# Splitting the first key load, loading small factors as rows and dropping zero rows in a fused attention and mixing kernel

## The chip, the cores and the metric

The program runs on one core of one Trainium2 chip. The metric is the device time of one execution in microseconds (us). A core has five engines that run their own lists of instructions in order: TensorE (PE; its weight loads are shown apart as PEld), VectorE (DVE), ScalarE (ACT), GpSimd (POOL) and SyncE (SP), which here only issues transfers. ScalarE issues a few transfers too.

## The reference

Three layers follow one another on batch B = 2, sequence S = 768, width 512:

```python
# 1. attention in hash buckets: 8 heads of 64, proj is 64 x 6
q_bits = (einsum('bhsd,dk->bhsk', q, proj) > 0)        # k_bits likewise
mask = q_bucket[:, :, :, None] == k_bucket[:, :, None, :]
scores = where(mask, scale * q @ k^T, -1e9)
x = softmax(scores) @ v                                # heads side by side
# 2. four attention experts of 64, causal, the two best per token, weighted
out += mask * w[:, :, kk] * (softmax(causal(q_e @ k_e^T)) @ v_e @ wo[e])
# 3. mixing with the token before
xk = mu_k * x + (1 - mu_k) * x_prev;  xr = mu_r * x + (1 - mu_r) * x_prev
k = max(xk @ w_k, 0);  out = sigmoid(xr @ w_r) * (k * k @ w_v)
```

## The kernel before

The tokens are cut into 12 tiles of 128 (6 per batch). For each tile the kernel makes the hash attention over 8 heads (`lsh_steps`), the experts (`moe_steps`) and the mixing (`mix_steps`). All numbers are split into a high and a low float16 part, and a product is made of two or three float16 products that add up in PSUM.

**Keys.** `key_steps` (from line 457) loads the keys of a group of four heads in two halves of two heads (`half(j)`), 384 KB each. ScalarE makes the high part and VectorE the low part into the tile `nak`, GpSimd puts a copy of the scaled keys into the first 64 columns of each 128 in the tile `nbk`. `turn` (line 338) transposes `nak` on TensorE in groups of six blocks of 128 x 128, and ScalarE and VectorE evict the results into `y2`. `hash_` multiplies `y2` with the projection (`hash_signs`) and `mark` writes 12 columns per block into `nbk`: a large number where a bit differs, else zero. The other 52 columns are filled with zeros by GpSimd. `nbk` is then transposed into `y1`. Queries go the same way (`query_steps`, tiles `naq`, `nbq`, `x2`, `x1`). A score is the sum of a product of `x1` with `y1` and one of `x2` with `y2`, each over 128 rows and twice 384 columns.

**Constants.** The projection is loaded twice, into rows 0 to 63 and 64 to 127 of `pr32`. The mixing factors `muk` and `mur` (128 x 4 each) are loaded with the partition as the inner index of memory, so every element is a piece of 4 bytes. They are first used when the first tile comes to the mixing, long after the start.

**Order.** The program is recorded first (class `Program`, line 151): every call of an engine becomes an operation, and consecutive TensorE calls of one step become one group. Then `issue` (line 203) makes all calls in the order of a table, `ORDER`, which holds one number per operation (2,594) and stands compressed in the source; `HOMES` holds the buffer of every tile. Both were written by a planner outside. As all calls go through line 208, the profile shows that line for all; the tiles' names tell them apart. Each engine takes its instructions from this order; SyncE and ScalarE issue their transfers in it.

The first transfers in the table of before are, on ScalarE's queue, the constants, the projection, `muk`, `mur`, the projection again and later `ties`; on SyncE's queue the queries of tile 0, three of the four first key halves, a weight load (128 KB of wq), the fourth key half, and more weight loads.

Of the kernel before, what the change touches and what calls it, by code (L numbers as in the profile page):

```python
# [42 lines left out]

KE, QE = {(0, 0): "va", (0, 1): "va"}, {}
# [191 lines left out]
def tile_lsh_moe_mix(  # L236
# [18 lines left out]
    G = 4  # L255
# [3 lines left out]
    NB2, NB3, NB4, NX2 = 40, 13, 2, 4  # L259

# [45 lines left out]
    nc.scalar.dma_start(pr32[0:64, :], proj)  # L306
    nc.scalar.dma_start(pr32[64:128, :], proj)
# [88 lines left out]
    def split_d(src, dst, sc, nm):  # L396
# [5 lines left out]
        top = raw[:, :, 1]  # L402
        nc.gpsimd.tensor_scalar(top.bitcast(F32), top.bitcast(F32), REBIAS, 1.0, op0=OP.mult, op1=OP.mult)
        w = dps(f"wd_{nm}", [P, n])
        u = w.bitcast(U32)
        nc.scalar.activation(u, raw.bitcast(U8)[:, :, 3], AF.Copy, bias=-15.5 / 32, scale=1.0 / 32)
        nc.vector.scalar_tensor_tensor(u, top, 3, u, op0=OP.logical_shift_left, op1=OP.bitwise_or)
        nc.vector.scalar_tensor_tensor(u, top, 0x80000000, u, op0=OP.bitwise_and, op1=OP.bitwise_or)
# [48 lines left out]
    def key_steps(b, g):  # L457
# [28 lines left out]
        def hash_():  # L486
# [24 lines left out]
    def query_steps(i):  # L511
# [16 lines left out]
        def hash_():  # L528
# [4 lines left out]
            turn(x1, nb.rearrange("p h c -> p (h c)"), f"x1_{i}", i in QD, QE.get(i, "vv"))  # L533
# [23 lines left out]
    def softmax(Sv, n, scale, sm, bias, nm, masked=None, by_pe=None):  # L557
# [6 lines left out]
        if masked:  # L564
            nc.vector.tensor_scalar(dst, Sv, masked, None, op0=OP.min, op1=OP.min, accum_out=bias)
            nc.vector.tensor_scalar(bias, bias, scale, None, op0=OP.mult)
        else:
            nc.vector.tensor_scalar(dst, Sv, -scale, None, op0=OP.mult, op1=OP.min, accum_out=bias)
        nc.scalar.activation(Pt, Pt, AF.Exp, bias=bias, scale=-scale if masked else -1.0, accum_out=sm)
        hi_part(hi_engine(), PHL[:, :n], Pt)  # L570
        lo_part("p", PHL[:, n:], Pt, PHL[:, :n])
        if by_pe:
            nk = n // P
            for j, eng in enumerate(by_pe):
                pt = dps(f"tp{j}_{nm}").bitcast(F16)[:, :n]
                for c in range(nk):
                    nc.tensor.transpose(pt[:, c * P:(c + 1) * P], PHL[:, j * n + c * P:j * n + (c + 1) * P], ident16)
                o = PT[:, j * nk:(j + 1) * nk, :]
                pt = pt.rearrange("p (t s) -> p t s", s=P)
                if eng == "a":  # L580
                    nc.scalar.activation(o, pt, AF.Copy)
                else:
                    nc.vector.tensor_copy(o, pt)
            return PT
        nc.sync.dma_start_transpose(PT, PHL)
        return PT
# [6 lines left out]
    def lsh_steps(i, LAG):  # L593
        b, t0 = divmod(i, NT)
        st = {"pt": {}}

        def score(h):
# [13 lines left out]
            st["pt"][h] = softmax(Sp[:, :, :HS], S, -0.125 / (SQ * SK), st["sm"][:, h:h + 1],  # L611
                                  st["mx"][:, h:h + 1], f"{i}_{h}", MASKED, SD.get((i, h)))
# [413 lines left out]
```

## Time and profile before

| | us |
|---|---|
| median of 3 runs | 457.49 (456.91 to 458.01) |
| profiled execution | 457.76 |
| its span (first to last instruction) | 455.9 |
| PE busy | 419.4 (92%) |
| PEld busy | 319.4 (70%) |
| DVE busy | 348.9 (77%) |
| ACT busy | 351.3 (77%) |
| POOL busy | 323.9 (71%) |

The profile is of one execution. Busy time is an average over stages that are bound by different engines, so the stages and the waits have to be read beside it. The granted TensorE clock is 1.00 in most stretches and lower in 30 to 60 us; its mean over the span is 0.985.

### The profile page before, as it was taken

The page shows a single profiled execution, that of the slowest core. Times are in us where ns is not written, and L with a number is a line of the kernel's source. Part 1 is how long each engine was busy: PE and PEld are TensorE (multiplying, and loading weights), DVE is VectorE, ACT ScalarE, POOL GpSimd, SP SyncE. Part 2 cuts the span into 40 slices and gives each one's busy share as a digit, 9 for nine tenths or more (in the row PEclk, how much of TensorE's full clock was granted, in tenths as well). Part 3 has the DMA queues.
Part 4 walks back from the last instruction along what each step waited for, and adds up shares of the span by engine and source line. Part 5 has one row for each costly group of instructions (what it writes and reads, how often), then busy time and mean ns, then how long its engine had stood idle before and what let it go on. Part 6 is the DMA issues. An engine that isn't in the chain of part 4 may idle for free.

```text
span 455.9 us, 15155 instructions
## 1 busy us (share of the span) xinstructions
PE 419.4 (92%) x6080; PEld 319.4 (70%) x6080; DVE 348.9 (77%) x994; ACT 351.3 (77%) x678; POOL 323.9 (71%) x321
## 2 busy tenths in 40 slices
PE   2765788899999999999999999999999999999996
PEld 2643566678767788687877778777768679866662
DVE  3899999999999789999787778867758537761513
ACT  4798999999999889689968978988597766552311
POOL 5599899999878876979989578689567844253020
PEclk9996799999999999999999999999999999999999
DMA  8999989899999999978999969997979975162003
GB/s 226 237 264 228 188 205 196 176 216 201 212 214 199 189 160 199 207 155 175 187 161 193 167 130 196 155 179 123 193 133 139 180 134 130 33 138 47 24 1 138
DMA packets 227158, 75.55 MB, mean 166 GB/s; under 512 B 218512, under 2 KB 222736, under 8 KB 227088
## 3 DMA queue, kind: packets, MB, share of 16 engines
q1 hardware_dynamic: 225584, 74.48, 84.3%
q8 instruction: 47, 0.77, 0.7%
q10 hardware_dynamic: 1504, 0.11, 0.3%
q14 instruction: 23, 0.19, 0.1%
HBM read 22.14 MB, written 3.15 MB: 55 GB/s over the span
## 4 chain that ended last, share of the span: by engine, by line
PE 66%; DVE 17%; DMA 6%; issue 5%; ACT 4%; POOL 1%; SPq 0%; DVEq 0%; ACTq 0%; POOLq 0%
PE h L208 13%; PE v L208 12%; PE s L208 8%; PE x L208 8%; PE r L208 6%; DVE P L208 5%; PE qk L208 5%; DMA PT<-PHL 3%; PE se L208 3%; PE vg L208 3%; PE o L208 3%; PE y L208 3%; DVE x L208 1%; DMA k<-in_k_dram 1%; DVE y L208 1%
## 5 line engine op out<-in xcount | busy, mean ns | idle before, releaser
L208 POOL TENSOR_TENSOR PHL<-P,PHL 128x768 f16<-128x768 f32 x96 | 159.4, 1672 | 26.8 <-ACT PHL L208 18.2
L208 DVE TENSOR_SCALAR_CACHE_REDUCE P<-s 128x768 f32<-128x768 f32 x96 | 90.9, 949 | 11.6 <-PE s L208 8.5
L208 ACT ACTIVATE P<-P,mx 128x768 f32<-128x768 f32 x96 | 89.0, 928 | 5.7 <-DVE mx L208 4.7
L208 PE MATMUL s<-y,x 128*128 128x384 f16 x384 | 78.2, 332 | 3.7 <-DVE P L208 2.4
L208 PE MATMUL h<-mk,WK 128*128 128x128 f16 x1152 | 74.5, 219 | 0.2 <-DVE x L208 0.2
L208 PEld LDWEIGHTS <-WK 128*128 128x128 f16 x1152 | 67.5, 98 | 6.0 <-issue 1.1
L208 PE MATMUL x<-v,PT 128*128 128x64 f16 x1728 | 63.5, 194 | 2.8 <-DMA PT<-PHL 1.4
L208 PEld LDWEIGHTS <-PT 128*128 128x128 f16 x1728 | 59.1, 99 | 8.3 <-DMA PT<-PHL 2.1
L208 ACT ACTIVATE PHL<-P 128x768 f16<-128x768 f32 x72 | 59.6, 837 | 5.7 <-DMA PT_m<-PHL_m 1.7
L208 PEld LDWEIGHTS <-x 128*128 128x128 f16 x480 | 38.7, 99 | 26.4 <-issue 7.0
L208 PE MATMUL v<-WV,k2h 128*128 128x512 f16 x192 | 57.1, 379 | 0.0
L208 POOL TENSOR_TENSOR PHL_m<-P_m,PHL_m 128x512 f16<-128x512 f32 (+2 forms) x24 | 34.6, 1452 | 8.1 <-ACT PHL_m L208 7.5
L208 PE MATMUL qk<-xT,WQK 128*128 128x128 f16 x576 | 36.3, 219 | 1.0 <-DVE xT L208 0.5
L208 PE MATMUL v<-WV,k2l 128*128 128x512 f16 x96 | 36.4, 379 | 0.0
L208 PEld LDWEIGHTS <-WQK 128*128 128x128 f16 x576 | 33.3, 98 | 2.8 <-issue 0.9
L208 PE MATMUL r<-WR,mr 128*128 128x512 f16 x144 | 35.0, 379 | 0.0
L208 POOL TENSOR_TENSOR mk<-m32k,mk 128x512 f16<-128x512 f32 x12 | 15.0, 1247 | 24.0 <-ACT mk L208 24.0
L208 DVE SCALAR_TENSOR_TENSOR h<-h,t 128x512 f32<-128x512 f32 x24 | 16.6, 693 | 19.5 <-ACT t L208 19.4
L208 ACT ACTIVATE t<-h 128x512 f32<-128x512 f32 x24 | 14.1, 586 | 17.1 <-PE h L208 17.1
L208 PEld LDWEIGHTS <-k2h 128*128 128x128 f16 x192 | 16.9, 98 | 13.0 <-DVE nbq L208 0.3
L208 ACT ACTIVATE P_m<-P_m,bias_m 128x512 f32<-128x512 f32 (+2 forms) x24 | 19.7, 822 | 7.4 <-DVE P_m L208 7.1
L208 POOL TENSOR_SCALAR PHL<-P 128x768 f16<-128x768 f32 x24 | 20.7, 863 | 4.4 <-ACT P L208 4.0
(146 smaller groups left out, 866.3 us busy)
## 6 DMA issues: line engine op xcount, KB each, us to landing
raw_k<-in_moe_w_k_dram SPq DMA_DIRECT2D x8, 512.0 KB, 4.2
raw_v<-in_moe_w_v_dram SPq DMA_DIRECT2D x8, 512.0 KB, 4.7
q<-in_q_dram SPq DMA_DIRECT2D x12, 256.0 KB, 4.7
k<-in_k_dram SPq DMA_DIRECT2D x8, 384.0 KB, 5.4
v<-in_v_dram SPq DMA_DIRECT2D x8, 384.0 KB, 4.9
out_dram<-e SPq DMA_DIRECT2D x12, 256.0 KB, 2.6
raw_r<-in_moe_w_r_dram SPq DMA_DIRECT2D x4, 512.0 KB, 4.6
PT<-PHL SPq DMA_TRANSPOSE x88, 4.3
```

The lines of the kernel that those rows point to most:

```text
L208: getattr(getattr(self.nc, engine), method)(*[real(a) for a in args], **{k: real(a) for k, a in kw.items()})
```

## The change

1. The first half of the keys (batch 0, group 0, half 0) is loaded, split into its high part and into its low part head by head: two transfers of 192 KB, two activations and two VectorE instructions in place of one each.
2. The projection is loaded once, through a view that repeats it.
3. `mu_k` and `mu_r` are loaded as four rows of 128 numbers each into one tile of eight rows, transposed on TensorE in one float32 product, and copied into one tile `mus`, of which `muk` and `mur` are the halves.
4. The keys' tiles are no longer filled with zeros. The transposes of `nbk` and `nbq` on TensorE take 76 columns (64 + 12) of each block, their evictions write 76 partitions, and the score products of `x1` and `y1` run over 76 rows.
5. `ORDER` and `HOMES` are new, for 2,590 operations. The first transfers in the new table are, on ScalarE's queue, the projection, the constants, `ties`, the rows of `mu_k`, then four activations (second, first and third key load used, the queries between), then the rows of `mu_r`; on SyncE's queue the second half of group 0's keys, the first half of group 1's, the queries of tile 0, the second half of group 1's, the two pieces of the first half of group 0's, then a weight load (wv), the queries of tile 1 and further weight loads.

Two switches, `PAIR` (empty) and `PRELU` (False), add branches that aren't taken; they are left out below, as are the tables.

```diff
+    KR = D + 2 * NB
...
-    nc.scalar.dma_start(pr32[0:64, :], proj)
-    nc.scalar.dma_start(pr32[64:128, :], proj)
+    nc.scalar.dma_start(pr32, proj.unsqueeze(0).to_broadcast([2, D, NB]))
...
-    muk = cp.tile([P, NC], F32, name="muk")
-    mur = cp.tile([P, NC], F32, name="mur")
+    mus = cp.tile([P, 2 * NC], F32, name="mus")
+    muk, mur = mus[:, :NC], mus[:, NC:]
...
-        nc.scalar.dma_start(muk, mu_k.rearrange("(c p) -> p c", p=P))
-        nc.scalar.dma_start(mur, mu_r.rearrange("(c p) -> p c", p=P))
+        rows = sp.tile([P, P], F32, tag="b2", bufs=NB2, name="mu_rows")
+        nc.scalar.dma_start(rows[0:NC, :], mu_k.rearrange("(c p) -> c p", p=P))
+        nc.scalar.dma_start(rows[NC:2 * NC, :], mu_r.rearrange("(c p) -> c p", p=P))
+        pt = dps("tr_mu", [P, P])
+        nc.tensor.transpose(pt[:, :2 * NC], rows[0:2 * NC, :], ident32[0:2 * NC, 0:2 * NC])
+        nc.vector.tensor_copy(mus, pt[:, :2 * NC])
...
-    def turn(dst, src, nm, by_dma=False, engs="vv"):
+    def turn(dst, src, nm, by_dma=False, engs="vv", kr=P):
...
-                nc.tensor.transpose(pt[j][:, c * P:(c + 1) * P], src[:, (j * hn + c) * P:(j * hn + c + 1) * P], ident16)
-            o, pj = dst[:, j * hn:(j + 1) * hn, :], pt[j].rearrange("p (n s) -> p n s", s=P)
+                nc.tensor.transpose(pt[j][:kr, c * P:(c + 1) * P], src[:, (j * hn + c) * P:(j * hn + c) * P + kr], ident16)
+            o, pj = dst[:kr, j * hn:(j + 1) * hn, :], pt[j][:kr].rearrange("p (n s) -> p n s", s=P)
...
-            LOADS.dma_start(k32, k[b, h0 + 2 * j:h0 + 2 * j + 2].rearrange(
-                "h (p t) d -> p h t d", t=NT))
...
-            kh = na[:, :, :, D:]
-            hi_part("a", kh, k32, SK)
-            lo_part("v", na[:, :, :, :D], k32, kh, SK)
+            cuts = [slice(r, r + 1) for r in range(2)] if (b, g, j) == (0, 0, 0) else [slice(0, 2)]
+            for r in cuts:
+                LOADS.dma_start(k32[:, r], k[b, h0 + 2 * j + r.start:h0 + 2 * j + r.stop].rearrange(
+                    "h (p t) d -> p h t d", t=NT))
+            for r in cuts:
+                kh = na[:, r, :, D:]
+                hi_part("a", kh, k32[:, r], SK)
+                lo_part("v", na[:, r, :, :D], k32[:, r], kh, SK)
             hi_part("p", nb[:, :, :, :D], k32, SK)
-            nc.gpsimd.memset(nb[:, :, :, D + 2 * NB:], 0.0)
+            if (b, g) in KD:
+                nc.gpsimd.memset(nb[:, :, :, KR:], 0.0)
...
-            turn(x1, nb.rearrange("p h c -> p (h c)"), f"x1_{i}", i in QD, QE.get(i, "vv"))
+            turn(x1, nb.rearrange("p h c -> p (h c)"), f"x1_{i}", i in QD, QE.get(i, "vv"), KR)
...
-                for a, (x, y) in enumerate((("x1", "y1"), ("x2", "y2"))):
-                    nc.tensor.matmul(Sp[:, n, :HS], QX[i][x][:, h, :], kg[y][:, hh, n * HS:(n + 1) * HS],
+                for a, (x, y, rows) in enumerate((("x1", "y1", slice(0, KR)), ("x2", "y2", slice(0, P)))):
+                    nc.tensor.matmul(Sp[:, n, :HS], QX[i][x][rows, h, :], kg[y][rows, hh, n * HS:(n + 1) * HS],
                                      start=(a == 0), stop=(a == 1))
```

`KD` is empty, so no key tile is filled with zeros; the transposes of `nbk` take `KR` in the same way as those of `nbq` (not shown).

## Rows read from the trace of the kernel before

**Rows 1.** Stages: window, length, busy us of PE, PEld, DVE, ACT, POOL; clock, DMA.

```profile
30.00:60.00 30.00, 19.23 (x240) 13.62 (x237) 29.16 (x64) 26.65 (x50) 26.59 (x23) 0.77 0.95 200
...
60.00:100.00 40.00, 34.53 (x555) 27.40 (x555) 38.34 (x119) 38.02 (x83) 37.38 (x38) 1.00 1.05 209
...
100.00:140.00 40.00, 37.27 (x604) 29.64 (x602) 39.65 (x122) 39.00 (x80) 35.24 (x39) 1.00 1.00 205
...
140.00:200.00 60.00, 59.33 (x940) 46.69 (x939) 52.73 (x146) 51.66 (x98) 49.10 (x51) 1.00 1.00 186
...
300.00:400.00 100.00, 100.00 (x1520) 77.15 (x1517) 67.25 (x198) 73.67 (x144) 64.04 (x61) 1.00 0.76 136
```

**Rows 2.** Chain of waits, first 20 us: start us, us, what.

```profile
4.68 5.99 DMA k<-in_k_dram
...
12.99 0.33 PE z_k L208 x6
```

**Rows 3.** Time line of ScalarE: start, us, operation, [idle before].

```profile
2.37 0.53 ACTq L208 DMA_DIRECT2D mur<-in_moe_mu_r_dram  x1
...
7.55 0.84 ACT L208 ACTIVATE nak<-k 128x768 f16<-128x768 f32 x1 [0.29 <-DMA k<-in_k_dram]
...
8.30 0.61 ACT L208 ACTIVATE naq<-q 128x512 f16<-128x512 f32 x1
...
10.69 0.84 ACT L208 ACTIVATE nak<-k 128x768 f16<-128x768 f32 x1 [0.94 <-DMA k<-in_k_dram]
```

**Rows 4.** Waits of SyncE, 0 to 60 us: total us, times, longest.

```profile
SPq L208 <- DMA q<-in_q_dram: 1.3, 1, 1.3
...
SPq L208 <- DMA muk<-in_moe_mu_k_dram: 1.0, 1, 1.0
```

**Rows 5.** Transfers issued before 25 us: count, KB, median us to landing.

```profile
pr<-in_proj_dram ACTq DMA_DIRECT2D x2, 1.5 KB, 4.9
...
muk<-in_moe_mu_k_dram ACTq DMA_DIRECT2D x1, 2.0 KB, 6.0
...
mur<-in_moe_mu_r_dram ACTq DMA_DIRECT2D x1, 2.0 KB, 7.0
```

**Rows 6.** Transfers, 4 to 8 us: all; ACT queue's packets, MB, share.

```profile
DMA packets 2175, 1.16 MB, mean 291 GB/s; under 512 B 1478, under 2 KB 2175, under 8 KB 2175
...
q10 hardware_dynamic: 1079, 0.01, 15.0%
```

**Rows 7.** VectorE: two rows of its time line, one group (busy, ns).

```profile
7.29 0.96 DVE L208 SCALAR_TENSOR_TENSOR nak<-k,nak 128x768 f16<-128x768 f32 x1 [7.29 <-ACT nak L208]
...
10.84 0.68 DVE L208 SCALAR_TENSOR_TENSOR naq<-q,naq 128x512 f16<-128x512 f32 x1
...
L208 DVE RECIPROCAL rs<-rs 128x8 f32<-128x8 f32 x12 | 2.3, 193 | 0.1
```

**Rows 8.** GpSimd: the fills by form, and a row of its time line.

```profile
L208 POOL MEMSET nbk<- 128x624 f16 x8 | 4.9, 617 | 0.4 <-POOLq L1010 0.3
...
13.80 0.64 POOL L208 TENSOR_SCALAR raw_k<-raw_k 128x512 f32<-128x512 f32 x1 [2.92 <-DMA raw_k<-in_moe_w_k_dram]
```

**Rows 9.** TensorE: products and weight loads by form; one row of the chain.

```profile
L208 PE MATMUL s<-y,x 128*128 128x384 f16 x384 | 78.2, 332 | 3.7 <-DVE P L208 2.4 <-ACT y L208 0.9 <-DVE x L208 0.2
...
L208 PE MATMUL se<-kT,qT 64*128 64x384 f16 x72 | 7.4, 325 | 0.3 <-DVE kT L208 0.3
...
L208 PEld LDWEIGHTS <-nbk 128*128 128x128 f16 x96 | 6.2, 99 | 1.5 <-issue 0.8 <-POOL PHL_m L208 0.4
...
L208 PEld LDWEIGHTS tr_x<-ident,x 128*128 128x128 f32 x32 | 3.4, 141 | 1.1 <-DVE x L208 1.0
...
383.45 0.67 PE h L208 x12
```

**Rows 10.** One wait of TensorE, 60 to 150 us; landing of the stored transposes.

```profile
PE tr_x L208 <- DVE yT L208: 1.1, 1, 1.1
...
PT<-PHL SPq DMA_TRANSPOSE x88, 4.3
```

More of the change, by code (lines that the diff above doesn't have):

```diff
@@ L41, in HP @@
     return n % 8 < 2
+PAIR, PRELU = (), False
 KE, QE = {(0, 0): "va", (0, 1): "va"}, {}
@@ L401, in split_d @@
         LOADS.dma_start(raw.rearrange("p n a -> p (n a)"), src.bitcast(U32))
-        top = raw[:, :, 1]
-        nc.gpsimd.tensor_scalar(top.bitcast(F32), top.bitcast(F32), REBIAS, 1.0, op0=OP.mult, op1=OP.mult)
         w = dps(f"wd_{nm}", [P, n])
         u = w.bitcast(U32)
-        nc.scalar.activation(u, raw.bitcast(U8)[:, :, 3], AF.Copy, bias=-15.5 / 32, scale=1.0 / 32)
-        nc.vector.scalar_tensor_tensor(u, top, 3, u, op0=OP.logical_shift_left, op1=OP.bitwise_or)
-        nc.vector.scalar_tensor_tensor(u, top, 0x80000000, u, op0=OP.bitwise_and, op1=OP.bitwise_or)
+        if PRELU:
+            end = sp.tile([P, n], U32, tag="b2", bufs=NB2, name=f"we_{nm}")
+            nc.gpsimd.tensor_scalar(end, raw.bitcast(U8)[:, :, 3], 1.0 / 32, -15.5 / 32, op0=OP.mult, op1=OP.add)
+            nc.scalar.activation(w, raw.bitcast(F32)[:, :, 1], AF.Prelu, scale=REBIAS, alpha=-(2.0 ** 32))
+            nc.vector.scalar_tensor_tensor(u, u, 3, end, op0=OP.logical_shift_left, op1=OP.bitwise_or)
+        else:
+            top = raw[:, :, 1]
+            nc.gpsimd.tensor_scalar(top.bitcast(F32), top.bitcast(F32), REBIAS, 1.0, op0=OP.mult, op1=OP.mult)
+            nc.scalar.activation(u, raw.bitcast(U8)[:, :, 3], AF.Copy, bias=-15.5 / 32, scale=1.0 / 32)
+            nc.vector.scalar_tensor_tensor(u, top, 3, u, op0=OP.logical_shift_left, op1=OP.bitwise_or)
+            nc.vector.scalar_tensor_tensor(u, top, 0x80000000, u, op0=OP.bitwise_and, op1=OP.bitwise_or)
         hi, lo = dst(0), dst(1)
@@ L565, in softmax, with rest @@
             nc.vector.tensor_scalar(dst, Sv, masked, None, op0=OP.min, op1=OP.min, accum_out=bias)
-            nc.vector.tensor_scalar(bias, bias, scale, None, op0=OP.mult)
+            if not paired:
+                nc.vector.tensor_scalar(bias, bias, scale, None, op0=OP.mult)
         else:
             nc.vector.tensor_scalar(dst, Sv, -scale, None, op0=OP.mult, op1=OP.min, accum_out=bias)
[L569 to L583, printed above, removed]
-            return PT
-        nc.sync.dma_start_transpose(PT, PHL)
-        return PT
+        def rest():
+            nc.scalar.activation(Pt, Pt, AF.Exp, bias=bias, scale=-scale if masked else -1.0, accum_out=sm)
+            hi_part(hi_engine(), PHL[:, :n], Pt)
+            lo_part("p", PHL[:, n:], Pt, PHL[:, :n])
+            if by_pe:
+                nk = n // P
+                for j, eng in enumerate(by_pe):
+                    pt = dps(f"tp{j}_{nm}").bitcast(F16)[:, :n]
+                    for c in range(nk):
+                        nc.tensor.transpose(pt[:, c * P:(c + 1) * P], PHL[:, j * n + c * P:j * n + (c + 1) * P], ident16)
+                    o = PT[:, j * nk:(j + 1) * nk, :]
+                    pt = pt.rearrange("p (t s) -> p t s", s=P)
+                    if eng == "a":
+                        nc.scalar.activation(o, pt, AF.Copy)
+                    else:
+                        nc.vector.tensor_copy(o, pt)
+                return PT
+            nc.sync.dma_start_transpose(PT, PHL)
+            return PT
+        return rest if paired else rest()
     NS = [0]
@@ L607, in score @@
             for n in range(2):
-                for a, (x, y) in enumerate((("x1", "y1"), ("x2", "y2"))):
-                    nc.tensor.matmul(Sp[:, n, :HS], QX[i][x][:, h, :], kg[y][:, hh, n * HS:(n + 1) * HS],
+                for a, (x, y, rows) in enumerate((("x1", "y1", slice(0, KR)), ("x2", "y2", slice(0, P)))):
+                    nc.tensor.matmul(Sp[:, n, :HS], QX[i][x][rows, h, :], kg[y][rows, hh, n * HS:(n + 1) * HS],
                                      start=(a == 0), stop=(a == 1))
-            st["pt"][h] = softmax(Sp[:, :, :HS], S, -0.125 / (SQ * SK), st["sm"][:, h:h + 1],
-                                  st["mx"][:, h:h + 1], f"{i}_{h}", MASKED, SD.get((i, h)))
+            rest = softmax(Sp[:, :, :HS], S, MSC, st["sm"][:, h:h + 1],
+                           st["mx"][:, h:h + 1], f"{i}_{h}", MASKED, SD.get((i, h)), i in PAIR)
+            if i not in PAIR:
+                st["pt"][h] = rest
+            elif h % 2 == 0:
+                st["rest"] = rest
+            else:
+                mx = st["mx"][:, h - 1:h + 1]
+                nc.vector.tensor_scalar(mx, mx, MSC, None, op0=OP.mult)
+                st["pt"][h - 1], st["pt"][h] = st["rest"](), rest()
         def pv(h):
@@ L983 @@
+>Is54_vBfzIp(uxOmgB$UJ-14dQwi;ENb*ois~*i#M4~V)}-+0Lj?pNTbjxt))}A0-sz-(H0vlnF4H_mY*_t8{+(>%Tq6@aC~miT?^ci158fopg2gEqmeeGa
+Qjj>KSH`6OJ*rG~j#eSxc-U&6`BH2}R4%#DE2DDI&og3wu2Ls*3#V;S;3gLNC|3egQK3P9wO(;GX3991-9DOP;`LgX)fp<X9nvB__BXrpW>@S2S$&<YIB6$+
+f(#!XDPOc)NR5TD7haFV&rB&^HFlP+ozar%!t*I0o2Tk_J!N@RhirH*GazHWH6puAM^x0+rwnSl8XB4^-onNYk=0p3pY_(!>!S%!v93gIcaidYO!nAUyh-V>
+JnXs%9)mQ{(_WJ333Aic>NSj(8AD{%wEsJKg6|2lyNj84w_x06&pdsr_PEnd$@2?25FJS
 """
```

109 lines of the change are left out of this document (53 added, 56 removed).

## The prediction

> **What bounds the kernel now.** I read four views, in this order: the busy time of the engines by stage, the chain of waits, the time line of the first 20 us, and the groups by form.
>
> The stages come first, because the answer differs by stage [rows 1]. From 140 us on TensorE is the bound: it works 59.33 of 60 us in 140 to 200 and all of 300 to 400. Anything saved there on another engine is worth nothing, and a stall put into TensorE's list there costs its full length. Before 140 us TensorE waits: 19.23 of 30 us busy in 30 to 60. There VectorE is the fullest: 29.16 of 30, 38.34 of 40, 39.65 of 40 us in the three stages. Its idle time in these 110 us is 0.84 + 1.66 + 0.35 = 2.85 us, so no order of the work can win more than that there without taking VectorE work out. So the end comes earlier only if VectorE starts its dense stretch earlier, has less to do before TensorE takes over, or loses some of the 2.85 us.
>
> The chain of waits then shows what that start hangs on [rows 2]: a load of keys, issued at 4.68 us and ending 5.99 us later, then ScalarE, then at 12.99 us the hash of the keys. This load is the fourth of the first four key loads, and in the time line ScalarE sits idle for it from 9.75 to 10.69 us (0.94 us), after 0.29 us for an earlier one [rows 3].
>
> **The change part by part.**
>
> (1) *Which load goes when.* In the kernel before, SyncE issues q, three key loads, then a weight load of 128 KB, then the fourth key load. SyncE's list stops several times for loads that aren't its own neighbours: 1.3 us for q, 1.0 us for muk [rows 4]. A load waits for the landing of the one issued eight before it, counted over both queues; the slow muk and mur therefore hold up SyncE's later loads as well. They land 6.0 and 7.0 us after their issue although they are 2 KB each, because they go as 1,024 pieces of 4 bytes [rows 5]. In 4 to 8 us the ACT queue's 1,079 packets took 15.0% of 16 engines, that is 0.15 x 16 x 4 / 1,079 = 8.9 ns each, and the whole moved 291 GB/s [rows 6]. The change puts 131 KB less ahead of the last key piece (the weight load now stands behind it): 0.131 MB / 0.291 MB per us = 0.45 us. The 1,024 small packets become 8; shared over 16 engines they took 64 x 8.9 ns = 0.57 us of each. So I put the landing of the last piece at 10.67 - 0.45 - 0.57 = 9.65 us. That is just before ScalarE would be ready for it (9.75), and the idle 0.94 us goes. The next thing late is ScalarE itself, with no idle left but the 0.29 us.
>
> (2) *What ScalarE gets in return.* One of its two new row loads, mur's, stands in ScalarE's list between the third and the last key piece: an issue takes 0.53 us [rows 3]. What is queued behind it is the split of the last keys and the two evictions of the first transposes, and the hash waits for those. It waits for nothing that isn't landed by then, and if the last piece is late it lies in that wait; so 0 to 0.53. The split of one key activation in two costs a start-up: 768 columns take 0.84 us and 512 take 0.61 [rows 3], 0.09 us per 100 columns, so 384 columns are an estimated 0.50 and the pair costs 0.16 us more. These 0.16 us and part of the issue eat the 0.29 us that ScalarE still idles. Also, the list takes the second load's keys first, and 128 KB more lie ahead of that load than before: up to 0.45 us later, less the small packets that are gone. So parts 1 and 2 together: between -1.23 us (both idles go, nothing paid) and 0; I take -0.94, the idle for the last load, since that wait ended last in the chain.
>
> (3) *VectorE's extra work.* The low part of the split keys in two: 0.96 us at 768 columns, 0.68 at 512 [rows 7], an estimated 0.54 at 384, so +0.12 us. The copy of the turned factors, 128 x 8: the nearest row is the reciprocal of 128 x 8, 0.19 us [rows 7], and I take 0.17. Both stand in the stretch in which VectorE is full, so both are on the path: +0.29 us (0.1 to 0.4).
>
> (4) *The zero rows.* Eight fills of the keys' tiles on GpSimd, 0.617 us each, 4.9 us in all [rows 8]. After the four early ones GpSimd waits 2.92 us for a weight load, to 13.80 us [rows 8]; they are covered. The other four come when TensorE is the bound. Worth 0 (down to -0.6, one fill, if the new list puts the weight load's landing earlier and GpSimd becomes late).
>
> (5) *76 rows in place of 128.* Of the 768 score products 384 run over 76 rows. A product over 64 rows and 384 columns takes 325 ns, over 128 rows 332 [rows 9]: rows don't set the time, 0. The transposes of the marked keys (96) and of the queries of tiles 0 to 7 (64) load 76 columns of weights in place of 128. A load of 128 columns takes 99 ns and hides under the products; the slow kind in this trace, float32, takes 141 ns and keeps the loader busy 3.4 us / 32 = 106 ns each [rows 9]. I take 0. At worst the narrow load is of the slow kind: 76 / 128 x 106 = 63 ns against 0.67 us / 12 = 56 ns for a product of 128 columns in the full stage [rows 9], so 7 ns on each; the 64 transposes that stand after 140 us (the second batch's keys and tiles 6 and 7) make +0.45 us.
>
> The Trainium skill ("TensorE: Matmul & The Clock Gate", section on the weight-path perf modes) says that the fast weight load is on only when the number of weights is 128 and the type isn't float32. By that rule the narrow loads are of the slow kind and the sum would be 0.45 us higher; the trace agrees as to float32 and shows nothing of 76 columns.
>
> (6) *The turn of the factors on TensorE*, one product in float32 before 30 us, where TensorE waits for others anyway: 0.
>
> (7) *The new order.* All lists are rewritten, but locally: in VectorE's list the normalising product of query tile 3 moves from place 275 to 276, of tile 5 from 417 to 420; in TensorE's list the gate projection of tile 4 from group 240 to 241. The stages therefore stay where they are; I take 0. The bounds: -2.85 us (all idle of VectorE gone) and, on the other side, stalls in TensorE's stage as costed below.
>
> The sum: -0.94 + 0.29 = -0.65 us. The profiled execution takes 457.76 us, 455.9 of it the span and 1.86 around it; 457.76 - 0.65 = 457.1. It is 0.27 above the median of the runs shown, 457.49, so against that the forecast is **456.8 us**.
>
> **The rivals.**
>
> *The order wins too.* VectorE or ScalarE lose most of the 2.85 us of idle time besides the head's gain. For: the list was remade with shorter loads at the start, and the idles in 30 to 100 us are many small ones. Against: they need the operands of four engines to fall well. Price -0.65 - 1.7 = -2.35: 455.1 us.
>
> *The head's gain is spent.* ScalarE is late by the issue and the split (0.53 + 0.16) and the first key load used lands 0.4 us later. For: only 0.29 us of its idle is left as a cushion. Then -0.94 + 0.69 + 0.29 = 0.04: 457.5 us.
>
> *The projection's load is confined.* It becomes one load whose outer dimension is a broadcast of 2. If its 128 pieces go to two engines, each carries 64 of them, 0.57 us by the price of part 1, which is what muk and mur cost every engine before; a key load lands with its slowest engine, so only the 0.45 us remain: -0.45 + 0.29 = -0.16, 457.3 us. Against: the two old loads of 1.5 KB landed in 4.9 us at the median [rows 5] and nothing in them shows an uneven share.
>
> The Trainium skill ("DMA: Bandwidth & Descriptors", its list of advice, the entry on using all 16 engines) states such a rule: a leading zero-stride broadcast of c copies confines the load to at most c engines. By it this rival would hold.
>
> *Slower: a stall in TensorE's stage.* TensorE takes its list in order. If the new list puts a group ahead of its operand after 140 us, the wait is paid in full. The nearest single wait is 1.1 us for VectorE (before 140 us); a stored transpose takes 4.3 us to land [rows 10]. Two waits of 1.1 us: -0.65 + 2.2 = +1.55, 459.0 us. It decides from 0.65 us of such waits on. For: every list is new. Against: before, the stage has only 0.67 us of waits in 140 to 200 and none in 300 to 400 [rows 1], with the same amount of work ahead of each tile.
>
> **How the numbers follow.** A run of this kernel can be told from no change at about 0.2%, 0.9 us. Forecast 0.42 (0.18 of it more than 0.9 us faster, 0.24 within); order wins 0.22 (faster); gain spent 0.12 (0.10 within, 0.02 slower); confined load 0.05 (within); stall 0.19 (slower). That is faster 0.40, same 0.39, slower 0.21. The range runs from 454.6 to 458.9: it takes in the bounds of the forecast, most of the order's case and the smaller stalls.
>
> **What would show it.** Right: the fourth key's last piece lands before 9.8 us, the hash of the first keys begins by 12.2, and the end of VectorE's dense stretch moves by about the same. Part 2 is wrong if ScalarE's gap around the row load is over 0.6 us, part 5 if narrow loads last clearly over 99 ns, part 7 if TensorE's busy share after 140 us falls below 99%. The prediction falls if the time moves by more than 2 us with the head unmoved.

## The result, and the profile after

The changed kernel is slower: 463.03 us median of 4 runs (462.53 to 465.7) against 457.75 of the kernel before beside it, a ratio of 1.013 (1.0087 to 1.0172). Measured a second time, in another batch, it came to 1.0124 (1.0088 to 1.0159). The forecast was 456.8 with a range to 458.9; the time lies outside it and on the other side. The profiled execution took 462.64 us, with a span of 460.9 against 455.9.

The stages of the kernel after, with the columns of [rows 1]:

```profile
30.00:60.00 30.00, 18.21 (x199) 12.62 (x198) 29.86 (x69) 26.84 (x49) 27.66 (x27) 0.83 0.87 196
60.00:100.00 40.00, 34.76 (x568) 27.83 (x568) 38.30 (x117) 37.64 (x80) 36.29 (x37) 1.00 1.03 205
100.00:140.00 40.00, 35.77 (x572) 27.95 (x567) 38.78 (x118) 37.69 (x80) 35.40 (x39) 1.00 1.00 188
140.00:200.00 60.00, 59.28 (x956) 46.43 (x954) 52.28 (x147) 50.69 (x94) 47.11 (x46) 1.00 1.03 196
300.00:400.00 100.00, 100.00 (x1548) 77.55 (x1545) 65.54 (x200) 76.11 (x145) 68.35 (x66) 1.00 0.83 147
```

Read against [rows 1], the stage behind 140 us looks the same: TensorE works 59.28 of 60 us (59.33 before) and all of 300 to 400. Ahead of 140 us TensorE has done less in two of the three stages (18.21 for 19.23, 35.77 for 37.27), while VectorE is about as full as it was. So the loss must lie earlier, or in what TensorE still has to do at 140 us. Two windows show both. The kernel before, then the kernel after (window, length, busy us of PE, PEld, DVE, ACT, POOL; clock, DMA, GB/s):

```profile
0.00:40.00 40.00, 22.69 (x250) 17.39 (x251) 31.11 (x73) 29.85 (x51) 27.44 (x36) 0.93 0.95 239
140.00:464.00 324.00, 311.30 (x4480) 234.88 (x4478) 220.63 (x638) 227.71 (x437) 205.59 (x195) 1.00 0.77 141
```

```profile
0.00:40.00 40.00, 21.68 (x237) 16.56 (x237) 29.04 (x73) 28.50 (x49) 24.03 (x30) 0.91 0.91 232
140.00:464.00 324.00, 315.84 (x4560) 238.50 (x4557) 223.22 (x649) 231.94 (x442) 206.61 (x193) 1.00 0.81 144
```

VectorE has worked 2.07 us less by 40 us, and TensorE has 4.54 us more left to do at 140 us. The span is 5.0 us longer.

**Where the 2 us go in the head.** The loads did come earlier, as forecast, but what follows them did not. ScalarE's time line of the kernel after (start, us, operation, [idle before]) shows the split key pieces and the row load:

```profile
8.64 0.26 ACTq L209 DMA_DIRECT2D mu_rows<-in_moe_mu_r_dram  x1
9.72 0.94 ACT L209 ACTIVATE nak<-k 128x384 f16<-128x384 f32 x2 [0.24 <-DMA k<-in_k_dram]
12.18 0.81 ACT L209 ACTIVATE y<-tr_y 128x768 f16<-128x768 f16 x1 [0.82 <-PE tr_y L209]
```

The pieces are in work by 9.72 us, and the row load, issued while the activation before it still ran, cost ScalarE no gap. Then TensorE, the same columns:

```profile
13.92 0.75 PE L209 MATMUL z_k<-prhl,y 128*128 128x12 f16 x24
...
16.17 0.80 PE L209 MATMUL tr_y<-consts,nbk 128*76 128x128 f16 x6 [0.71 <-DVE nbk L209]
...
19.40 0.65 PE L209 MATMUL tr_x<-consts,nbq 128*76 128x128 f16 x4 [0.98 <-POOL nbq L209]
...
20.56 1.46 PE L209 MATMUL s<-y,x 76*128 76x384 f16 x4
```

The hash of the first keys (group 1 of batch 0, in both kernels) begins at 13.92 us; in the kernel before it began at 10.97 and its last part stood at 12.99 [rows 2]. Those keys' second half is now the fourth load on SyncE's queue instead of the third, and stands fourth in ScalarE's list instead of second. Then the marked queries come late from GpSimd. Its time line in the kernel after says why:

```profile
13.34 0.62 POOL L209 TENSOR_SCALAR w_qk<-w_qk 128x512 f32<-128x512 f32 x1 [1.12 <-DMA w_qk<-in_moe_wq_dram]
15.69 0.65 POOL L209 TENSOR_SCALAR raw_k<-raw_k 128x512 f32<-128x512 f32 x1 [1.73 <-DMA raw_k<-in_moe_w_k_dram]
18.04 0.62 POOL L209 TENSOR_SCALAR w_qk<-w_qk 128x512 f32<-128x512 f32 x1 [1.70 <-DMA w_qk<-in_moe_wq_dram]
18.72 0.62 POOL L209 TENSOR_SCALAR nbq<-q 128x512 f16<-128x512 f32 x1
```

The scaling of the first queries (0.62 us) stood at 8.04 us before. In the new order it stands behind three scalings of weights, each of which waits for its load. GpSimd waits 4.55 us for loads here, in three pieces, where it waited 2.92 in one [rows 8]; worse than the length is what is queued behind. VectorE pays. What its idle time in 14 to 40 us waited for (us in total, times, longest), kernel before, then after:

```profile
DVE x L208 <- PE tr_x L208: 0.5, 1, 0.5
DVE y L208 <- PE tr_y L208: 0.4, 1, 0.4
DVE P L208 <- PE s L208: 0.2, 1, 0.2
```

```profile
DVE x L209 <- PE tr_x L209: 1.8, 2, 1.4
DVE P L209 <- PE s L209: 1.0, 1, 1.0
DVE y L209 <- PE tr_y L209: 0.5, 1, 0.5
DVE z_k L209 <- ACT zl_k L209: 0.3, 1, 0.3
```

1.1 us became 3.6. One more thing stands in the windows of the kernel before and of the kernel after (columns as above):

```profile
16.00:20.00 4.00, 3.20 (x43) 2.55 (x42) 3.18 (x11) 3.45 (x7) 2.63 (x6) 1.00 0.94 292
20.00:24.00 4.00, 3.04 (x50) 2.19 (x47) 3.99 (x13) 4.00 (x9) 2.83 (x3) 1.00 0.78 192
```

```profile
16.00:20.00 4.00, 2.84 (x27) 2.52 (x28) 2.09 (x7) 3.23 (x7) 2.16 (x4) 0.53 1.08 237
20.00:24.00 4.00, 4.00 (x49) 2.88 (x46) 2.63 (x6) 1.83 (x4) 2.44 (x4) 0.62 0.92 244
```

VectorE falls from 7.17 to 4.72 us in these 8 us. The granted clock of TensorE is 0.53 and 0.62 here, mostly the lower of its two levels (1.2 of 2.4 GHz), where it was 1.00 before; four score products take 1.46 us instead of 0.81. Ahead of it, in 12 to 16 us, TensorE had worked 2.72 us, against 3.49 in the kernel before. Whether the low clock or the waits cost VectorE more is taken up below, with the second measurement of this kernel.

### The profile page after: what moved, and what is told of

Its sections match the earlier page's. It is cut to its first block, busy times and chain, and to the rows that moved or that the text cites. A ratio compares the mean times of both kernels' runs of the same rounds, so it can differ in the third digit from the quotient of the medians.

```text
span 460.9 us, 15143 instructions
## 1 busy us (share of the span) xinstructions
PE 421.9 (92%) x6081; PEld 320.6 (70%) x6081; DVE 349.2 (76%) x996; ACT 352.7 (77%) x679; POOL 321.0 (70%) x313
## 4 chain that ended last, share of the span: by engine, by line
PE 49%; POOL 2%; DMA 1%; ACT 1%; issue 0%; DVE 0%; DVEq 0%; POOLq 0%
PE v L209 11%; PE h L209 10%; PE s L209 6%; PE r L209 5%; PE x L209 5%; PE qk L209 3%; PE o L209 2%; PE y L209 2%; PE vg L209 2%; PE se L209 2%; POOL PHL L209 1%; DMA PT<-PHL 1%; ACT P L209 0%; PE tr_x L209 0%; PE tr_y L209 0%
## 5 line engine op out<-in xcount | busy, mean ns | idle before, releaser
L209 POOL TENSOR_TENSOR PHL<-P,PHL 128x768 f16<-128x768 f32 x96 | 161.1, 1686 | 30.6 <-ACT PHL L209 27.7
L209 PE MATMUL s<-y,x 76*128 76x384 f16 (+1 forms) x384 | 79.9, 335 | 4.7 <-DVE P L209 3.2
L209 PEld LDWEIGHTS <-x 76*128 76x128 f16 (+1 forms) x480 | 39.0, 100 | 26.7 <-issue 8.7
L209 POOL TENSOR_TENSOR mk<-m32k,mk 128x512 f16<-128x512 f32 x12 | 13.9, 1159 | 25.3 <-ACT mk L209 25.1
```

The source lines that it names most:

```text
L209: getattr(getattr(self.nc, engine), method)(*[real(a) for a in args], **{k: real(a) for k, a in kw.items()})
```

## Experiments

The theory after the result: the edits are worth about what was forecast, and the new order loses 5 to 6 us, most of it by local moves in the head that delay VectorE. The rivals: the edits themselves cost (the 76-column weight loads, the split), or the stage behind 140 us stalls. Ratios are to runs of the kernel before taken beside each kernel; 1% is 4.58 us.

### Edits against order

All edits in the order of before, only the new instructions given places of their own; then the opposite, the kernel before in the changed order:

```diff
 # parts_old_order: table of before, with
-ACT load muk; ACT load mur;  SP load k(0,0,0);  8 x POOL memset nbk
+ACT load rows of mu_k; ACT load rows of mu_r;  SP load k(0,0,0) head 0, head 1
 PE  s(0,0)
+PE  turn of the rows
 # new_order_alone: table of after, with the old loads, splits and fills
```

> All four edits of the change (split key load, one hash load, factors as rows, no zero fill), carried out in the order of the kernel before; the only new places are those of the new instructions. Order theory (the edits are cheap, the new order costs): 456.0 to 457.5, faster than before or level with it. Edits theory (the 76-column weight loads, 126 ns against 99, and the split with its extra instructions cost): 460 or more, in the direction of the changed kernel's 463.

Measured: 458.17 us beside 458.98 of before, 0.9967 (0.9943 to 0.9992).

> None of the edits: the kernel before with its whole key load, its two hash loads, its column loads of the factors and its zero fills, all put into the changed kernel's order. Order theory: 462 to 465, as slow as the changed kernel or slower. Edits theory: 457 to 459, near before.

Measured: 462.65 us, 1.0080 (1.0055 to 1.0105). The order alone makes the kernel slower by 3.7 us, without any of the edits; the edits alone make it no slower. The edits theory falls. With an order comes its table of buffers, `HOMES`: in new_order_alone, as in the kernel after, 921 of 1,276 tiles stand in other buffers than before. No run has the one without the other, so "order" means both tables here. Both kernels were measured again with others, unaltered:

> All four edits in the order of before, unaltered from the first run of it, as the reference for the three beside it: 456.5 to 458.5, 0.3 to 1.5 below before.

Measured: 458.52 beside 458.66, 0.9993 (0.9972 to 1.0015). The first 0.9967 was on the good side; the mean of the two is 0.998, 0.9 us.

> The changed kernel once more, unaltered, as the reference for the three beside it: 462.5 to 465 if the first measurement holds.

Measured: 464.36 us, 1.0124, and in its profiled execution the head lost still more (VectorE 26.71 us by 40 us). The changed kernel runs from 461.67 to 466.97. Its two profiled executions, of the same tables, run alike on TensorE up to 13.6 us. Then one group of eight products, first in the kernel after, then in after_again:

```profile
25.71 1.48 PE L209 MATMUL s<-y,x 76*128 76x384 f16 x8
```

```profile
26.86 2.76 PE L209 MATMUL s<-y,x 76*128 76x384 f16 x8
```

The second is at the speed of the lower clock level, although the clock column shows 1.00 there. In the kernel after, products and transposes have that speed from 16.2 to about 23 us, in after_again from 13.7 to about 29. Order, buffers and edits are the same, and yet VectorE has done 2.33 us less by 40 us and the span is 2.6 us longer. So the time that TensorE spends at the lower level is part of the head's loss, beside the waits. No run holds it fixed, and how much of the loss it makes up stays open.

TensorE's rows for the first hash in parts_old_order:

```profile
9.97 0.33 PE L209 MATMUL z_k<-prhl,y 128*128 128x12 f16 x6
11.04 0.48 PE L209 MATMUL z_k<-prhl,y 128*128 128x12 f16 x12 [0.75 <-ACT y L209]
11.74 0.33 PE L209 MATMUL z_k<-prhl,y 128*128 128x12 f16 x6 [0.22 <-ACT y L209]
```

The last part comes at 11.74, against 12.99 in [rows 2]: the head's gain is real, 1.25 us in this execution, as long as the order doesn't spend it.

### Where along the list the order loses

Each of these kernels has all four edits and takes a first stretch of one order and the rest of the other:

```diff
 # after_head_old_rest: 215 steps of after's table, the others as in before's
 # old_head_after_rest: 215 steps of before's table, the others as in after's
 # old_to_60, old_to_100, old_to_140: 336, 500, 730 steps of before's table, then after's
 # old_from_140: 730 steps of after's table, then before's
```

> All four edits; the first 215 steps of the list (to about 42 us) in the changed kernel's order, all others in the order of before. If the loss is made in the head: 460.5 to 463. If it is made in the rest: 456 to 458. If the head's delay is taken up by waits that stand behind it anyway: below 459.

Measured: 461.74, 1.0052 (1.0017 to 1.0088).

> All four edits; the first 215 steps in the order of before, all others in the changed kernel's order. If the loss is made in the head: 456 to 458. If the rest has it (the turn of the query tile ahead of its operand at 37 us, stalls behind 140 us): 460 to 463.

Measured: 461.44, 1.0054 (1.0017 to 1.0092). So neither half alone: the loss is spread.

> All four edits; the first 336 steps (to about 60 us) in the order of before, the others in the changed kernel's. If the loss is made before TensorE becomes the bound, in many places: 458.5 to 460.5, between the old head alone and the old order throughout, and TensorE's busy time behind 140 us stands as far above before's as the span does. If everything is lost in the first 60 us: 456 to 458.

Measured: 461.65, 1.0073 (1.0052 to 1.0095): not lower than with 215 steps, but the intervals overlap.

> As the one beside it, with the first 500 steps (to about 100 us) in the order of before. Many places before 140 us: 457 to 459, no higher than with 336 steps. Stalls behind 140 us: 460 or more still.

Measured: 459.86, 1.0038 (1.0020 to 1.0056).

> As the one beside it, with the first 730 steps (to about 140 us) in the order of before. If all of the loss is made ahead of 140 us, where VectorE is the bound: 456 to 458, level with the old order throughout. If the changed order's stalls in TensorE's own stage (the two waits of 0.6 and 0.5 us seen behind 140 us) cost: 1 to 3 more than that.

Measured: 459.19, 1.0016 (0.9993 to 1.0039).

> All four edits; the first 730 steps (to about 140 us) in the changed kernel's order, the others in the order of before. If the loss is made ahead of 140 us: 462 to 464, as slow as the changed kernel. If the order of the stage behind 140 us costs as well: 0.5 to 2 less than the changed kernel.

Measured: 462.94, 1.0080 (1.0051 to 1.0108).

From 0.998 (old order throughout) to 1.0127 (changed order, mean of two) there are 1.47%, 6.7 us. Each stage's share can be taken from either end. Up to 40 us: 1.0052 - 0.9980 = 0.72%, or 1.0127 - 1.0054 = 0.73%, so 3.3 us. Behind 140 us: 1.0016 - 0.9980 = 0.36%, or 1.0127 - 1.0080 = 0.47%, so 1.6 to 2.2 us. Between: what is left, 1.2 to 1.8 us. Each share is uncertain by 1.3 to 2.1 us: the head's stands clear of zero, the one behind 140 us barely, the one between not; that the two ends agree speaks for them. "Up to 40 us" means the first 215 steps.

Behind 140 us the traces show less than that. TensorE's idle time there (span, less 140, less its work) is 4.6 us in the kernel before and 5.1 in the kernel after. What TensorE waited for there in the kernel after:

```profile
PE z_k L209 <- DVE m32r L209: 0.6, 1, 0.6
PE s L209 <- DVE P_m L209: 0.5, 1, 0.5
```

The kernel before has one such wait, of 0.5 us, and old_from_140 none. That makes 0.6 us of the 1.6 to 2.2; the remainder, if it isn't the measurement's error, was not found.

### Single moves

```diff
 # queries_first: GpSimd's list of the kernel after
 POOL scale nbk(0,1,0)
+POOL scale nbq, tile 0
 POOL scale nbk(0,1,1), nbk(0,0,0)
 POOL scale w_qk01; scale raw_k21; scale w_qk00
-POOL scale nbq, tile 0
 # old_start: loads, splits and first hash (35 steps) as in before
 # old_start_queries: 43 steps as in before, nbq's scaling among them
 # turn_later: kernel after with
+DVE split naq_2
 DVE low parts of v_0_0, v_0_1
-DVE split naq_2
-PE  tr_x2_2 (two groups)
 PE  tp0_0_0, s_1_4, tp1_0_0, s_0_2
+PE  tr_x2_2 (two groups)
```

> The changed kernel with one step moved: GpSimd scales the first query tile right behind the second key tile, no longer behind a weight matrix whose load it waits for. If that wait (scaling at 18.72 in the changed kernel, 8.04 in the one before) is what the head loses: 460.5 to 461.5, 1.5 to 2.5 below the changed kernel's 463.0, with the first score product at 19.5 or earlier instead of 20.6. If the late hash (13.9 instead of 11.0) loses it: 462.5 to 463.5.

Measured: 462.23, 1.0085 (1.0053 to 1.0118), about 2 us better than the changed kernel by the ratios, but the intervals overlap, and the time lies in neither range. In its trace the first scores start at 19.97 us, not by 19.5, and four of them still take 1.46 us; VectorE has done 28.53 us by 40 us. That the one step makes the head's loss is not shown.

> The changed kernel with only its first 35 steps (loads and first splits, up to the hash of the first key group) in the order of before; the queries' scaling stays where the change put it. If the load order and the late hash make the head's loss: hash at 10.0 to 11.8 and 460.5 to 461.5. If the queries' scaling makes it: hash early, but the first scores at 20 or later and 462.5 to 463.5.

Measured: 462.79, 1.0082 (1.0056 to 1.0108). The hash came at 10.23 to 12.87 us, the first scores at 20.15 all the same, as in the second reading. By the ratio it, too, is 2 us better than the changed kernel, and again the intervals overlap.

> The changed kernel with its first 43 steps in the order of before (loads, first hash, and the queries' scaling ahead of the weights): the two single moves that gave 1.0082 and 1.0085 each, together. If they add: 459.5 to 461.5, as the old order up to 40 us (1.0054). If both remove the same loss: 462 to 463.

Measured: 462.34, 1.0083 (1.0051 to 1.0115). The two moves don't add. Its trace is nearly repaired up to 40 us:

```profile
16.00:20.00 4.00, 3.96 (x62) 3.68 (x60) 3.34 (x12) 2.99 (x6) 1.93 (x3) 1.00 1.11 277
20.00:24.00 4.00, 2.89 (x34) 2.13 (x31) 3.48 (x9) 3.54 (x7) 3.13 (x4) 1.00 0.68 183
```

VectorE is back at 6.82 us in these two windows, at 31.33 up to 40 us, and the clock is 1.00. The time is still 4.7 us above the old order, give or take 1.6 us, where the two later shares make 2.8 to 4.0; its interval overlaps that of old_head_after_rest, 1.0054. Whether the steps from 43 to 215 have a share of their own isn't settled.

The most striking wait of the changed kernel is TensorE's at 37 us, for the split of query tile 2. The row of the kernel after:

```profile
42.15 1.03 PE L209 MATMUL tr_x<-consts,naq 128*128 128x128 f16 x8 [5.21 <-DVE naq L209]
```

> The changed kernel with its turn of the third query tile moved behind the two score products and the two turns that it stood ahead of, and VectorE's split of that tile ahead of two value splits, as before. If TensorE's wait of 5.2 us at 37 is what the rest of the list loses: 460.5 to 461.5. If the loss of the rest is spread over many places: 462.5 to 463.5, with other waits in that wait's place.

Measured: 464.65, 1.0117 (1.0087 to 1.0148): no better. The wait is gone, and others stand in its place. TensorE's two longest waits of turn_later in 12 to 60 us:

```profile
PE s L209 <- DVE P L209: 3.7, 2, 3.3
PE tp L209 <- DVE WK L209: 2.5, 1, 2.5
```

Both end with VectorE; nine smaller ones, 7.3 us together, end with VectorE, ScalarE and GpSimd. In this stage TensorE's idle time is no cost by itself; it shows that VectorE is behind.

### Which engine passes a delay on

Work that changes nothing, added to parts_old_order:

```diff
 # vector_extra
 DVE reduction of the first scores
+DVE split of nak(0,0,1) once more, twice
 # tensor_extra
-PE  turn nbk(0,0,0), nbk(0,0,1): 4 groups of 6 transposes
+PE  the same, each group of 6 done twice
```

> The kernel beside it with two more instructions on VectorE, right behind its first score reduction at about 20 us: the split of a key tile done twice over, some 2.4 us of work that changes nothing. If VectorE's place on its list is what the stage up to 140 us runs by, and no wait behind it takes the delay up: 1.8 to 2.6 more than the reference. If there is slack: under 0.8 more.

Measured: 463.03 beside 458.52 of parts_again, 1.0091 (1.0055 to 1.0126) against 0.9993: 4.5 us more, give or take 1.9. VectorE's row for the addition:

```profile
21.43 3.59 DVE L209 SCALAR_TENSOR_TENSOR nak<-k,nak 128x768 f16<-128x768 f32 x2
```

3.59 us of VectorE, 120 us before TensorE becomes the bound, still cost at least 2.6 us at the end, 440 us later, and by the middle of the interval all of their length. Part of it may have gone through TensorE's speed: TensorE waited 3.30 us for VectorE here, and its granted clock was 0.69 and 0.50 in 24 to 28 and 28 to 32 us, where that of parts_again was 1.00.

> The kernel of the first run with 24 more transposes on TensorE between 21 and 28 us, four groups of six done twice, some 2.0 us of work that changes nothing. VectorE theory: under 1.0 more than the reference, since TensorE waits in that stretch anyway. If TensorE's own lateness in the head is what costs: 1.5 to 2.5 more.

Measured: 459.38, 1.0012 (0.9992 to 1.0033): 0.9 us more, give or take 1.4, for 24 transposes of some 63 ns (1.50 us for 24 in a row), 1.5 us. VectorE's work up to 40 us is 30.36 us, as in parts_again: the addition didn't reach it. That fits the VectorE theory, but the interval holds the full 1.5 us as well, so that an addition on TensorE costs less for its length is not shown.

The same can be looked for over all the kernels. VectorE's useful work up to 40 us, TensorE's work left at 140 us, and the span, each from one profiled execution:

| kernel | VectorE to 40 | TensorE behind 140 | span |
|---|---|---|---|
| loads_alone | 31.14 | 311.18 | 455.7 |
| before | 31.11 | 311.30 | 455.9 |
| parts_old_order | 31.23 | 312.16 | 456.4 |
| parts_again | 30.36 | 312.67 | 456.7 |
| narrow_alone | 29.62 | 313.71 | 457.7 |
| old_to_100 | 30.95 | 312.88 | 457.8 |
| old_head_after_rest | 31.40 | 312.90 | 457.9 |
| tensor_extra | 30.36 | 313.25 | 458.5 |
| old_to_140 | 30.96 | 313.74 | 458.5 |
| old_to_60 | 31.49 | 314.12 | 458.6 |
| old_from_140 | 30.52 | 314.91 | 458.8 |
| old_start_queries | 31.33 | 314.52 | 459.0 |
| after_head_old_rest | 30.61 | 315.41 | 459.4 |
| new_order_alone | 29.53 | 315.43 | 460.3 |
| after | 29.04 | 315.84 | 460.9 |
| old_start | 29.86 | 316.29 | 461.1 |
| queries_first | 28.53 | 317.42 | 462.4 |
| turn_later | 28.18 | 317.65 | 462.4 |
| after_again | 26.71 | 318.59 | 463.5 |
| vector_extra, less 3.59 | 26.04 | 317.96 | 463.8 |

The span is TensorE's work behind 140 us plus 143.9 to 145.8 in every row: TensorE is idle for 4 to 6 us there in all of them, and the rest of the difference was made earlier. What VectorE lacks at 40 us mostly shows up as TensorE's work at 140 us: the four kernels with the least are the four slowest. It is not the whole account. old_to_60 and old_start_queries lack nothing at 40 us and still have 2.8 and 3.2 us more left at 140 than the kernel before; they lose between 40 and 140 us.

### The edits apart

```diff
 # narrow_alone: before, with 76 rows for 128 in nbk, nbq, y1, x1; no fills
 # loads_alone: parts_old_order with 128 rows and the fills
```

> The kernel before, in its own order, with one edit: 76 rows instead of 128 in the hash parts, and no zero fills in the keys' tiles. If the slower weight loads (126 ns against 99) lie on the path: 457.9 to 458.2, 0.1 to 0.5 above before. If they are hidden: level with before, 457.3 to 457.8. If the freed GpSimd time starts something earlier: below 457.3.

Measured: 459.19 beside 458.72, 1.0019 (0.9994 to 1.0043).

> The order of before with three of the four edits: key load split, hash projection in one load, factors as rows; the hash parts stay 128 rows high and the zero fills stay. With the 76 rows alone measured at 1.0019 and all four at 0.9967 and 0.9993: if the earlier loads are worth the 1.0 us by which the first hash starts earlier, 456.8 to 458.0, 0.7 to 1.8 below before. If the first hash's gain is taken up later: level with before.

Measured: 457.11 beside 458.27, 0.9967 (0.9946 to 0.9988): 1.5 us faster than before, the best of all kernels here. The loads and the split are the gain; the 76 rows add nothing to it, and may take some away. The weight loads of the marked keys by form (count | busy us, mean ns of one | idle before), over the whole run, first of loads_alone, then of the kernel after:

```profile
L209 PEld LDWEIGHTS <-nbk 128*128 128x128 f16 x96 | 6.4, 102 | 1.4 <-issue 0.8 <-POOL PHL_m L209 0.4
```

```profile
L209 PEld LDWEIGHTS <-nbk 128*76 128x76 f16 x96 | 7.1, 126 | 1.5 <-issue 1.0
```

These means mix two speeds: in the first 30 us some of the loads ran at the lower clock level. The same two from 150 to 455 us, where the clock is 1.00:

```profile
L209 PEld LDWEIGHTS <-nbk 128*128 128x128 f16 x48 | 3.0, 98 | 0.8 <-POOL PHL_m L209 0.4 <-issue 0.3
```

```profile
L209 PEld LDWEIGHTS <-nbk 128*76 128x76 f16 x48 | 3.0, 115 | 0.0
```

At the same clock a load of 76 columns takes 115 ns where one of 128 takes 98. The loader's busy time for the 48 is the same, 3.0 us (3.1 in narrow_alone, whose loads take 115 ns too).

## Why the prediction was wrong

**Parts 1 and 2** (loads and ScalarE, -0.94): right in size, but not in their terms. With part 3's 0.29 for VectorE the forecast for these was -0.65; loads_alone measured -1.5 (-2.5 to -0.5). The order of before keeps the weight load ahead of the fourth key load, so the term of 0.45 us is not in this measurement. And ScalarE's idle 0.94 us for that load doesn't go: 0.57 us are left in parts_old_order, 0.58 in loads_alone. Its last key activation starts at 9.45 us in the one and at 10.06 in the other, 10.69 before. That the sum fits is partly luck. The row load on ScalarE cost no gap in the kernel after, below the 0.53 that was allowed for it. For part 3, the split pieces took VectorE 0.61 and 0.91 us (at 12.01 and 13.45) in the kernel after and 0.55 each in loads_alone, where 0.54 was estimated.

**Part 4** (fills, 0) wasn't measured apart from part 5. Part 6 was right in size: the turn took 0.22 us on TensorE and its copy 0.15 us on VectorE, where 0.17 was assumed.

**Part 5** (76 rows, 0, at worst +0.45): the products were right, 335 ns over 76 rows and 335 over 128 in the kernel after. The sign named for the worst case, a load over 99 ns, is there: 115 ns against 98. Its cost isn't seen: the loader's busy time behind 150 us is no longer with 76 columns than with 128. With the fills gone, narrow_alone measured +0.9 us (-0.3 to +2.0), which contains 0 and 0.45.

The Trainium skill ("TensorE: Matmul & The Clock Gate", section "Weight-path perf modes") says that the fast weight load is on when the number of weights is 128 and the type isn't float32. The trace agrees in that the narrow load is the slower one, 115 ns against 98.

**Part 7** (the new order, 0) is the step that failed. It was measured at +3.7 us without the edits (new_order_alone) and, between the old order and the new with all edits, at some 6.7 us. The evidence taken for it was the place of a few operations far down the lists, moved by one to three places, and the conclusion was that stages stay where they are. They do; but the head doesn't live by stages. There one operation of 0.62 us, moved behind waits for loads, holds TensorE for 0.98 us and VectorE for 1.44 us, and TensorE's clock falls to its lower level from 16 to 23 us, which the prediction didn't reckon with. The order as the cause is shown by the exchanged tables; which of its moves cost how much is not, as the single moves gave no difference clear of noise. The bound on the bad side was also put in the wrong place: stalls in TensorE's list behind 140 us. The prediction's first section had said that VectorE has 2.85 us of idle time in 110 us; the other reading of that number, that VectorE can't make good what it loses ahead of that stretch, was not drawn.

**The rivals.** "The order wins too" (0.22) is refuted. "The head's gain is spent" had the right direction but named ScalarE; in the trace GpSimd's list, the order of the keys and TensorE's clock spent it, and more. The slower case, two stalls behind 140 us, priced at 2.2 us, fits the share measured there (1.6 to 2.2) in size, but only 0.6 us of it is seen in the trace, and it is the smaller part of the loss.

The confined load of the projection has rows for it. The chain of waits in parts_old_order (start us, us, what) begins with that load, and the fourth key load stands behind it:

```profile
1.19 4.35 DMA pr<-in_proj_dram
...
5.56 3.87 DMA k<-in_k_dram
```

The 4.9 us of [rows 5] are the middle of two loads, 3.3 and 6.4 us; the one issued at 1.18 us took 3.3, and the kernel before issued its fourth key load at 4.68. So the single load takes about 1.1 us longer, and the key load goes out 0.9 us later. SyncE waits 1.0 us for it in parts_old_order and 2.3 in the kernel after. Whether it is slower because few engines carry it, no row shows; the edits with the projection still loaded in two halves were not tried.

**The signs.** In the kernel after the last two key pieces were in work at 9.72 and 10.15 us, the second without a wait, so the sign for the load (landed before 9.8) held or came close while the hash missed its own (13.92, not by 12.2). TensorE's share behind 140 us hardly moved, 59.28 of 60 for 59.33; a share of busy time doesn't tell how much work is left, so it was no test of part 7.

**Open.** The edits gain 0.9 us in the old order; in the new one they seem to cost (1.0080 without them, 1.0127 with them), but the intervals overlap, and no kernel tells it apart.

## What to carry to other kernels

When an order written out by a planner changes along with the edits, forecast it from each engine's list in the head: for every operation that waits for a load, name what is queued behind it and who waits for that. Where one engine has no idle time, what it lacks at the start of that stretch mostly comes back at the end, so ask of a stall on another engine whether it reaches this one. Ask also what a load that was put first holds up behind it. Test edits and order apart: the edits in the old order were the faster kernel here.

## What the runs showed of the hardware that was not expected

VectorE's split of a key tile (128 x 768) took 0.95 us at 11.93 us in vector_extra, and the two at 21.43 took 3.59 us together. GpSimd stood still at the first and ran two subtractions over the second, which took 2.98 us instead of 2.27 in parts_old_order. So each engine's work of this kind lasted longer while the other's ran, here by some 0.8 us per split; the added work came to 3.59 us rather than the 2.4 that was planned. A transposition to 76 columns is not cheaper than one to 128: behind 150 us, at clock 1.00, its weight load takes 115 ns instead of 98, and its product 220 ns in the kernel after, 219 in loads_alone.
